# Scales of the weights: one small operation a turn, and the values' maxima two steps sooner

## The chip, the cores and the metric

The kernel runs on one core of a Trainium2 chip. The metric is the device time of one execution in microseconds; the figure before is the median of three runs. Everything else is read from one profiled execution, whose own time stands in the table below. Engine names are those of the profile: PE multiplies matrices, DVE reduces and transposes, ACT exponentiates, POOL does element-wise work, SP issues most DMAs.

## The reference

Two attention blocks A and B over the same input, mixed row by row by a gate (S = 2048 rows, D = 640, 32 heads of 20):

```python
def block(x, wqkv, wo):
    q, k, v = split_heads(x @ wqkv)          # 32 heads of 20
    p = softmax(q @ k.T * 20 ** -0.5)
    return (p @ v).reshape(B, S, D) @ wo

g = sigmoid((x * gate_w).sum(-1, keepdims=True))
out = g * block(x, A_wqkv, A_wo) + (1 - g) * block(x, B_wqkv, B_wo)
```

## The kernel before

The 64 heads of both blocks are worked in 16 groups of four (g = 0 to 15). A group has four blocks of 512 queries, and each of these eight steps over the keys, so the main loop has 512 steps (G), some 5.2 us each; step G belongs to group G // 32. In a step PE makes eight score products (L672), which ACT exponentiates (L675), and two sets of eight value products into the one accumulator bank `acc` (L690), which DVE empties with a transpose `ot` (L777) every eighth step. Some 15 steps ahead of the scores PE makes the same products the other way round (L614), and DVE takes each row's maximum from them: six plain reductions a step (L625) and one fused operation (L622, two records), whose other half ACT has rectified first (L618). Products and their readers share seven PSUM banks. Beside this, the projections of later groups (L407) fill one or two slots a step.

Each weight block is split in two f16 halves after division by a power of two near its largest magnitude, so that maximum has to be known first. The chain that finds it runs three times for queries and keys (`scales_qk`), seven times for values (`scales_v`, one for each group pair gg = 1 to 7) and twice for the output weights (`scales_o`): twelve times in the main loop. It goes so:

- the weights are loaded into `wstage` (one of two buffers) and DVE takes each partition's maximum. For values this is one reduction of 128x800, `m` (L258); for the others it is pieces, `wmax`.
- `scales_by_dram` (L201 on): SP writes the 128 maxima to DRAM (L208), reads them back to every partition as `srows` (L212), and DVE reduces them to `es` (L216).
- `powers` (L165 on): four operations on `es` (L168 to L171) make the power of two and its inverse. The second and third each read what the one before wrote; the fourth reads the second's result.
- `then`: copies and products for the kind of chain. For values `r_v` (L233) and two or three pieces of `wrow` (L239); for queries and keys `r_qk` (L226) and three operations on `esc` (L228 to L230); for output weights `r_o` and two operations on `f_o` (L251 to L253).

The order of instructions on each engine is the order in which the Python code emits them. A chain is a generator on a list `side`; `advance()` moves every generator of it by one `yield`, and it is called eight times a step, after each score product. What stands between two yields is emitted as one piece. The table of future work is filled by `at(G, task)`; its tasks run in the middle of step G, after the fourth score product and ahead of the second set of value products. For values and group g = 2gg - 2, which begins at step b = 32g, the load is put at b - 9, the maximum at b - 6 and the split of the weights at b - 1. For gg = 1, whose b is 0, these are steps 0, 3 and 8, and for gg = 7 load and maximum come by a rule of their own, at 338 and 341. `take_acc`, which issues `ot`, runs right after the second set of value products of every step that 8 divides.

The banks are chosen by `take()`, which picks the bank that a running tally of engine times (`spend`, `tick_block`) holds to be free first. The tally counts 0.5 us for a maximum of weights and 0.35n + 0.5 us for a whole chain's tail, at the place of its `es` reduction.

Of the kernel before, what the change touches and what calls it, by code (L numbers as in the profile page):

```python
# [12 lines left out]
I32 = mybir.dt.int32  # L13
# [11 lines left out]
NT = S // P  # L25
# [46 lines left out]
def kernel(  # L72
# [73 lines left out]
    def give(i, t):  # L146
        free_at[i] = t
        held.discard(i)
# [7 lines left out]
    def tick_block(cost, ready=0.0):  # L156

        begin = block_end[0] if now[0] < 0 and block_end[1] == rows_free else max(rows_free) + T_MODE
        clock["pe"] = max(begin, ready)
        rows_free[:] = [clock["pe"] + cost + T_MODE] * 2  # L160
        block_end[:] = [clock["pe"] + cost, list(rows_free)]
        clock["done"] = clock["pe"] + cost + T_READY - T_MODE


    def powers(ei, n):  # L165

        c = [slice(k * n, (k + 1) * n) for k in range(5)]
        nc.vector.tensor_scalar(ei[:, c[1]], ei[:, c[0]], 0x7F800000, None, op0=OP.bitwise_and)  # L168
        nc.vector.tensor_scalar(ei[:, c[2]], ei[:, c[1]], float(20 << 23), None, op0=OP.max)
        nc.vector.tensor_scalar(ei[:, c[3]], ei[:, c[2]], -1.0, float((254 + XE) << 23), op0=OP.mult, op1=OP.add)  # L170
        nc.vector.tensor_scalar(ei[:, c[4]], ei[:, c[2]], float(XE << 23), None, op0=OP.subtract)  # L171

    def scales(maxima, n, then):

        for _ in range(REST):
            yield
        yield PRODUCT
        i, pt = take()
        nc.tensor.transpose(pt[:n, :P], maxima[:, :n], ident)
        tick_block(0.1, free_at[i])  # L180
        yield
        e = wts.tile([5, 8], F32, name="e", tag="scl", bufs=2)
        nc.vector.tensor_reduce(e[:n, 0:1], pt[:n, :P], axis=AX.X, op=OP.max)
        give(i, spend("dve", 0.3, clock["done"]))
        spend("dve", 1.0)
        powers(e.bitcast(I32)[:n, :], 1)
        dg = wts.tile([5, 10], F32, name="dg", tag="scd", bufs=2)[:n, :2 * n]
        nc.vector.tensor_tensor(dg.rearrange("p (k n) -> p k n", k=2), ident[:n, :n].unsqueeze(1).to_broadcast([n, 2, n]),
                                e[:n, 3:5].unsqueeze(2).to_broadcast([n, 2, n]), op=OP.mult)
        for _ in range(REST):  # L190
            yield
        yield PRODUCT
        i, pb = take()
        tick_block(0.1, free_at[i])
        nc.tensor.matmul(pb[:, :2 * n], ones[:n, :], dg, start=True, stop=True)
        yield
        both = wts.tile([P, 10], F32, name="both", tag="scb", bufs=2)
        nc.vector.tensor_copy(both[:, :2 * n], pb[:, :2 * n])
        give(i, spend("dve", 0.2, clock["done"]))
        then(both[:, :n], both[:, n:2 * n])  # L200

    def scales_by_dram(maxima, n, then):

        turn = next(scale_turns)
        flat = s_scr[turn % 3][:n * P]
        yield
        yield
        nc.sync.dma_start(flat.rearrange("(p n) -> p n", n=n), maxima[:, :n])  # L208
        for _ in range(STORED):
            yield  # L210
        rows = wts.tile([P, 2 * P], F32, name="srows", tag="srows", bufs=2)[:, :n * P]
        nc.sync.dma_start(rows, flat.unsqueeze(0).to_broadcast([P, n * P]))  # L212
        for _ in range(LOADED):
            yield
        e = wts.tile([P, 10], F32, name="es", tag="ses", bufs=2)
        nc.vector.tensor_reduce(e[:, :n], rows.rearrange("p (q n) -> p n q", n=n), axis=AX.X, op=OP.max)  # L216
        spend("dve", 0.35 * n + 0.5)
        powers(e.bitcast(I32), n)
        then(e[:, 3 * n:4 * n], e[:, 4 * n:5 * n])

    def set_x(r_x, r, inv):
        nc.vector.tensor_copy(r_x, r)
# [1 line left out]

    def set_qk(i, r, inv):
        nc.vector.tensor_copy(r_qk[i], r)  # L226
        e = esc[i]
        nc.vector.tensor_tensor(e, inv[:, 0:1], inv_x, op=OP.mult)  # L228
        nc.vector.tensor_scalar(e, e, inv[:, 1:2], float(DH ** -0.5 / QKS ** 2), op0=OP.mult, op1=OP.mult)
        nc.vector.tensor_tensor(e, e, inv_x, op=OP.mult)  # L230

    def set_v(gg, r, inv):
        nc.vector.tensor_copy(r_v[gg], r)  # L233

        f = gg % (NG // 2) * 160
        while f < (gg % (NG // 2) + 1) * 160:
            p0 = f % P
            n = min(P - p0, (gg % (NG // 2) + 1) * 160 - f, (P, 32, 64, 32)[p0 // 32])
            nc.vector.tensor_copy(wrow[gg // (NG // 2)][p0:p0 + n, f // P:f // P + 1], inv[p0:p0 + n])  # L239
            f += n  # L240

    def scales_qk(i, maxima):
# [6 lines left out]
    def scales_o(z, maxima):  # L249
        def then(r, inv):  # L250
            nc.vector.tensor_copy(r_o[z], r)  # L251
            nc.vector.tensor_scalar(f_o[z], gates[:, z, :], inv, inv_x, op0=OP.mult, op1=OP.mult)
            nc.vector.tensor_scalar(f_o[z], f_o[z], 1.0 / QKS, None, op0=OP.mult)  # L253

        return scales_by_dram(maxima, 1, then)
# [49 lines left out]
    side = []  # L305
# [139 lines left out]
    def run(gen):  # L445
        for _ in gen:
            pass
# [468 lines left out]
    load, split_next = weights_a(1)  # L916
# [4 lines left out]
    r, inv = found  # L921
# [72 lines left out]
    rv, invv = of_v  # L994
# [5 lines left out]
    run(r_chunk(1, (0, 1)))  # L1000

    def next_group():
        set_qk(0, r[:, 0:2], inv[:, 0:2])
        set_v(0, rv[:, 0:1], invv[:, 0:1])
        split_next()
        yield True

# [30 lines left out]
    todo, fill, current = {}, [], []  # L1038

    def at(G, f):  # L1040
        todo.setdefault(G, []).append(f)
# [5 lines left out]
    def tasks(G, gap, fs):  # L1047
        for k, f in enumerate(fs):
            at(G + k * gap, f)

    at(4, sigmoids)
    step = NQ * NS
    for g in range(2 * NG):
        b = g * step
        n = g + 1
        if n < 2 * NG:
            parts = APARTS.get(n, 3)
            fill += [((-8, 15)[g] if g < 2 else b + AFROM, b + ADUE + ADUES * ch if g else 4 + 3 * ch, parts, project_a(n, ch))
                     for ch in range(4)]
            if n + 1 < 2 * NG:  # L1060
                tasks(b + 2 if g else 9, 3, weights_a(n + 1))
            i = g // 4 + 1
            if i < 4:
                if g % 4 == 0:
                    z, c0 = i // 2, 320 * (i % 2)
                    srcs = max_tasks([[(wqkv[z], part * D + c0 + 160 * k) for k in range(2)] for part in range(2)],
                                     lambda m, i=i: scales_qk(i, m))
                    tasks(b + QKMAX[i], 2, srcs)
                if g % 4 == 2:
                    tasks(b + 6, 3, weights_r(i))  # L1070
                    parts = RPARTS.get(i, 3)
                    fill += [(b + 12, b + 26 + 6 * ch if i == 1 else b + 22 + 4 * ch, parts, project_r(i, ch)) for ch in range(4)]
            gg = g // 2 + 1
            if gg < NG and g % 2 == 0:
                load, scale, split = weights_v(gg)
                at(max(b - 9, 0), load)
                if gg < NG - 1:
                    at(max(b - 6, 3), lambda scale=scale: side.append(scale()))
                at(max(b - 1, 8), split)
                fill += [(max(b + 2, 10), b + 2 * step - 4 + j // 2, 2, project_v(gg, j)) for j in range(0, NT, 2)]  # L1080
    early = weights_v(NG - 1)
    at(VEARLY, early[0])
    at(VEARLY + 3, lambda: side.append(early[1]()))
# [89 lines left out]
    for G in range(STEPS + 1):  # L1173
# [13 lines left out]
        for what in (STEP[blocks] if maxima or some else LATE + " X" * (blocks == 2)).split():  # L1187
            k = count[what] = count.get(what, 0) + 1
            if what[0] == "e":
                q = sum(count.get(f"e{j}", 0) for j in range(2)) - 1  # L1190
                j = int(what[1])
# [55 lines left out]
```

## Time and profile before

| | |
|---|---|
| median of three runs | 2762.35 us (2762.08 to 2764.07) |
| the profiled execution | 2762.97 us |
| its span | 2761.2 us |
| PE, busy share of the span | 99% |
| ACT | 92% |
| DVE | 89% |
| POOL | 24% |

The profiled execution lies 0.62 us above the median and within the three runs. Its span is 1.8 us shorter than its time; nothing of that lies in the main loop. A start of a row is counted from the span's start. Two DVE operations may overlap by some hundredths in their records, since an operation's record goes on after the next one has begun; the distance of two starts is what one costs the engine. PE's records overlap likewise, so that PE counts as busy in places where it advances slowly; how far it advances is read from the starts of its rows. A set of value products is eight rows of L690, merged to one with x8.

### The profile page before, as it was taken

What the parts mean: (1) busy time and instruction counts of PE and PEld (TensorE: products, weight loads), DVE (VectorE), ACT (ScalarE), POOL (GpSimd) and SP (SyncE); (2) the same over time, 40 slices, a digit from 0 to 9 for tenths busy, and PEclk for the clock granted to TensorE, in tenths of its full rate; (3) what the DMA queues carried; (4) which work ended last, traced back from release to release, by engine and by line L of the source; (5) the groups of instructions that cost most, each with busy time, mean ns of one, the idle gap of its engine ahead of it and who ended that gap; (6) DMA issues with size and microseconds to landing.
All of it is one profiled execution on the core that took longest, in us unless ns stands there. A gap on an engine that the chain in (4) does not pass through costs nothing.

```text
span 2761.2 us, 62247 instructions
## 1 busy us (share of the span) xinstructions
PE 2722.8 (99%) x23273; PEld 935.9 (34%) x23273; DVE 2444.3 (89%) x4785; ACT 2528.5 (92%) x5128; POOL 667.0 (24%) x909
## 2 busy tenths in 40 slices
PE   7999999999999999999999999999999999999998
PEld 3433333333333332333333333333333333333222
DVE  7789899999999989888888998989988898999982
ACT  4999999999999999999999999999999999999987
POOL 6232222222123421311221111222342202100111
PEclk8999999999999999999999999999999999999999
DMA  4021102010120211102012230221201112132112
GB/s 143 16 57 26 31 11 47 7 31 16 25 55 20 60 42 49 43 9 61 20 45 62 60 85 25 60 56 48 65 17 42 30 50 63 32 78 63 47 48 76
DMA packets 176432, 125.58 MB, mean 45 GB/s; under 512 B 105216, under 2 KB 145976, under 8 KB 176128
## 3 DMA queue, kind: packets, MB, share of 16 engines
q1 hardware_dynamic: 173584, 119.99, 17.1%
q8 instruction: 182, 2.98, 0.5%
q0 software_dynamic: 1600, 0.96, 0.2%
q14 instruction: 122, 1.00, 0.1%
q10 hardware_dynamic: 944, 0.66, 0.1%
HBM read 55.53 MB, written 31.86 MB: 32 GB/s over the span
## 4 chain that ended last, share of the span: by engine, by line
PE 94%; DVE 4%; ACT 1%; DMA 1%; issue 0%; POOL 0%; POOLq 0%; SPq 0%; ACTq 0%; DVEq 0%
PE acc L690 35%; PE bank L407 20%; PE bank L614 20%; PE bank L672 18%; DVE mpart L625 2%; ACT pt L675 1%; DMA ws<-in_A_wqkv_dram 0%; PE bank L854 0%; DVE rl L622 0%; PE bank L900 0%; DVE ot L777 0%; DMA xs<-in_A_x_dram 0%; POOL wstage L336 0%; ACT rl L618 0%; DVE es L216 0%
## 5 line engine op out<-in xcount | busy, mean ns | idle before, releaser
L675 ACT ACTIVATE pt<-bank 128x512 f32<-128x512 f32 x4096 | 2168.5, 613 | 146.0 <-PE bank L672 98.0
L625 DVE TENSOR_REDUCE mpart<-bank 128x1 f32<-128x512 f32 x2944 | 1843.7, 682 | 220.4 <-PE bank L614 118.8
L690 PE MATMUL acc<-pt,v 128*21 128x512 f32 x8192 | 1081.7, 600 | 1.4 <-DVE ot L777 1.2
L672 PE MATMUL bank<-qt,kt 64*128 64x512 f16 x4096 | 1041.7, 380 | 4.6 <-DVE mpart L625 2.9
L614 PE MATMUL bank<-kt,qt 60*128 60x512 f16 x3520 | 1011.6, 380 | 4.2 <-ACT pt L675 1.3
L614 PEld LDWEIGHTS <-qt 60*128 60x128 f16 x4096 | 238.4, 94 | 883.4 <-issue 821.9
L622 DVE CUSTOM_DVE_ANT_0 rl<-bank,rl 128x512 f32<-128x512 f32 x576 | 388.1, 680 | 7.0 <-ACT rl L618 2.2
L618 ACT ACTIVATE rl<-bank 128x512 f32<-128x512 f32 x576 | 336.9, 594 | 7.1 <-PE bank L614 6.7
L672 PEld LDWEIGHTS <-kt 64*128 64x128 f16 x4096 | 230.2, 94 | 199.4 <-issue 88.5
L690 PEld LDWEIGHTS acc<-pt,v 128*21 128x21 f32 x8192 | 143.0, 99 | 431.9 <-issue 426.4
L407 PE MATMUL bank<-xx,wbh 128*128 128x168 f16 (+3 forms) x2480 | 287.7, 236 | 1.4 <-DVE wbh L926 1.0
L407 PE MATMUL bank<-xx,wbl 128*128 128x168 f16 (+3 forms) x1240 | 257.5, 235 | 0.0
L785 POOL TENSOR_TENSOR ot<-ot,sq 128x512 f32<-128x512 f32 x63 | 66.0, 1048 | 755.3 <-DVE sq L782 755.3
L407 PEld LDWEIGHTS <-wbh 128*128 128x128 f16 x2480 | 192.8, 98 | 110.8 <-issue 104.5
L614 PE MATMUL bank<-kd,qt 60*128 60x512 f16 x576 | 203.7, 379 | 0.1
L407 PE MATMUL bank<-woh,o_in 128*128 128x320 f16 (+3 forms) x700 | 157.7, 290 | 0.0
L407 PE MATMUL bank<-wvh,xx 128*128 128x160 f16 (+1 forms) x1280 | 156.7, 234 | 0.6 <-DVE mpart L622 0.6
L436 POOL CAST cq<-fs 128x512 f16<-128x512 f32 x60 | 36.6, 610 | 477.3 <-ACT fs L434 473.6
L407 PEld LDWEIGHTS <-xx 128*128 128x128 f16 x1920 | 131.1, 97 | 59.1 <-issue 56.3
L407 PE MATMUL bank<-wvl,xx 128*128 128x160 f16 (+1 forms) x640 | 137.7, 232 | 0.0
L407 PEld LDWEIGHTS <-wbl 128*128 128x128 f16 x1240 | 121.1, 98 | 4.7 <-issue 1.3
L407 PEld LDWEIGHTS <-o_in 128*128 128x128 f16 (+1 forms) x1050 | 87.3, 97 | 90.7 <-issue 68.8
(145 smaller groups left out, 1247.4 us busy)
## 6 DMA issues: line engine op xcount, KB each, us to landing
y_scr<-y_out SPq DMA_DIRECT2D x48, 320.0 KB
y_out<-y_scr SPq DMA_DIRECT2D x32, 320.0 KB
kt<-cq SPq DMA_DIRECT2D x120, 80.0 KB
o_scr<-on SPq DMA_DIRECT2D x240, 40.0 KB
o_in<-o_scr SPq DMA_DIRECT2D x64, 96.0 KB
kt<-cq SPq DMA_DIRECT2D x136, 40.0 KB
wstage<-in_B_wqkv_dram SPq DMA_DIRECT2D x13, 400.0 KB
xs<-in_A_x_dram SPq DMA_DIRECT2D x8, 640.0 KB
```

Source lines behind the costliest of these rows:

```text
L407: nc.tensor.matmul(out_ap, a, b, start=(k == 0), stop=(k == len(pairs) - 1))
L436: nc.gpsimd.tensor_copy(hi, f)
L614: nc.tensor.matmul(pt, QT[g % 2][r, pair, q0:q0 + P], k, start=True, stop=True)
L618: nc.scalar.activation(relus[u, j], pt, AF.Relu)
L622: nc.vector.tensor_tensor_reduce(rl, pt, rl, 1.0, LOW, OP.add, OP.max, m)
L625: nc.vector.tensor_reduce(m, pt, axis=AX.X, op=OP.max)
L672: nc.tensor.matmul(et, KT[g % 2][r, pair, kt * P:(kt + 1) * P], QT[g % 2][r, pair, qb * QB:(qb + 1) * QB], start=True, stop=True)
L675: nc.scalar.activation(pt, et, AF.Exp, scale=factor(g // 4))
L690: nc.tensor.matmul(acc[32 * h:32 * h + VW, :], V[(g // 2) % 2][:, kt, (g % 2) * GH + h, :], ptiles.pop((G, kk, h)), start=(kt == 0), stop= ...
L785: nc.gpsimd.tensor_tensor(t3, t3, sq.unsqueeze(2).to_broadcast([P, 16, 32]), op=OP.mult)
```

## The change

`powers` and each `then` yield after nearly every operation, so that a chain's tail of eight or nine operations is emitted over several turns of `advance()`, with other work between them. Calls at the start, outside the main loop, are run through at once as before. The values' load and maximum are put two steps sooner, and for gg = 1 the split and the projection it feeds are allowed two steps later.

```diff
         nc.vector.tensor_scalar(ei[:, c[1]], ei[:, c[0]], 0x7F800000, None, op0=OP.bitwise_and)
+        yield
         nc.vector.tensor_scalar(ei[:, c[2]], ei[:, c[1]], float(20 << 23), None, op0=OP.max)
+        yield
         nc.vector.tensor_scalar(ei[:, c[3]], ei[:, c[2]], -1.0, float((254 + XE) << 23), op0=OP.mult, op1=OP.add)
+        yield
         nc.vector.tensor_scalar(ei[:, c[4]], ei[:, c[2]], float(XE << 23), None, op0=OP.subtract)
+        yield
...
         spend("dve", 0.35 * n + 0.5)
-        powers(e.bitcast(I32), n)
-        then(e[:, 3 * n:4 * n], e[:, 4 * n:5 * n])
+        yield
+        yield from powers(e.bitcast(I32), n)
+        yield from then(e[:, 3 * n:4 * n], e[:, 4 * n:5 * n])
...
     def set_v(gg, r, inv):
         nc.vector.tensor_copy(r_v[gg], r)
+        yield
...
             nc.vector.tensor_copy(wrow[gg // (NG // 2)][p0:p0 + n, f // P:f // P + 1], inv[p0:p0 + n])
+            yield
...
-                at(max(b - 9, 0), load)
+                at(max(b - 11, 0), load)
                 if gg < NG - 1:
-                    at(max(b - 6, 3), lambda scale=scale: side.append(scale()))
-                at(max(b - 1, 8), split)
-                fill += [(max(b + 2, 10), b + 2 * step - 4 + j // 2, 2, project_v(gg, j)) for j in range(0, NT, 2)]
+                    at(max(b - 8, 3), lambda scale=scale: side.append(scale()))
+                at(max(b - 1, 10), split)
+                fill += [(max(b + 2, 12), b + 2 * step - 4 + j // 2, 2, project_v(gg, j)) for j in range(0, NT, 2)]
```

`set_qk` and `then` of `scales_o` have yields in the same manner.

What this does to the order of the engines, at three places. A row has the line, the operation and the tiles; lines of the change count from the changed file, so L216 there is L220, L258 is L270, L625 is L637, L622 is L634 and L777 is L789. `ISA` is the fused operation and the read of its result.

DVE, the tail of the chain of gg = 3, before (some 125 steps in):

```order
L625 TENSOR_REDUCE mpart<-bank_93 128x1
L216 TENSOR_REDUCE es<-srows 128x1
L168 TENSOR_SCALAR es<-es 128x1
L169 TENSOR_SCALAR es<-es 128x1
L170 TENSOR_SCALAR es<-es 128x1
L171 TENSOR_SCALAR es<-es 128x1
L233 COPY r_v_110<-es 128x1
L239 COPY wrow_115<-es 32x1
L239 COPY wrow_115<-es 128x1
L622 ISA rl,mpart<-bank_92,rl 128x512
```

DVE, the same tail in the change, from its third operation on (the reduction and three maxima stand ahead of it):

```order
L168 TENSOR_SCALAR es<-es 128x1
L170 TENSOR_SCALAR es<-es 128x1
L634 ISA rl,mpart<-bank_91,rl 128x512
L634 ISA mpart 128x1
L172 TENSOR_SCALAR es<-es 128x1
L174 TENSOR_SCALAR es<-es 128x1
L637 TENSOR_REDUCE mpart<-bank_95 128x1
L241 COPY r_v_110<-es 128x1
L248 COPY wrow_115<-es 32x1
L637 TENSOR_REDUCE mpart<-bank_89 128x1
L248 COPY wrow_115<-es 128x1
```

Eight operations in a row have become five groups of one or two, with one to three maxima between them, and the whole stands two steps sooner.

DVE, around the transpose of the accumulator eight steps ahead of gg = 3's group (step 120), in the change:

```order
L637 TENSOR_REDUCE mpart<-bank_93 128x1
L270 TENSOR_REDUCE m_9810<-wstage 128x1
L634 ISA rl,mpart<-bank_94,rl 128x512
L634 ISA mpart 128x1
L789 STREAM_TRANSPOSE ot<-acc 128x512
L794 RECIPROCAL sq<-ot 128x16
L637 TENSOR_REDUCE mpart<-bank_89 128x1
```

Before, `m` stood two steps later, and these rows stood here without it. Since b - 8 is divisible by eight, `m` now comes in the step of `ot`, directly ahead of it, for gg = 2, 3, 4, 5 and 6.

DVE, the same place for gg = 4 (step 184), in the change:

```order
L270 TENSOR_REDUCE wmax<-wstage 128x1
L270 TENSOR_REDUCE m_14336<-wstage 128x1
L637 TENSOR_REDUCE mpart<-bank_92 128x1
L637 TENSOR_REDUCE mpart<-bank_95 128x1
L634 ISA rl,mpart<-bank_91,rl 128x512
L634 ISA mpart 128x1
L270 TENSOR_REDUCE wmax<-wstage 128x1
L789 STREAM_TRANSPOSE ot<-acc 128x512
L794 RECIPROCAL sq<-ot 128x16
```

Here `m` joins the last two pieces of the queries' and keys' maxima; they stood here before, `m` did not. Further on, the chain of gg = 4 and that of queries and keys i = 2, which followed each other without a row between them, are a step and a half apart.

On PE and ACT the order of instructions is the same in both kernels; only which bank a product takes differs, and whose product had that bank before differs in five short stretches, where `m` has moved. On POOL the split of gg = 1 comes five rows later. On SP the load of `wstage` comes one to three rows sooner in two places, and the read of `srows` directly behind the write of the maxima, ahead of the DMAs of the row maxima (L646, L650), in four.

More of the change, by code (lines that the diff above doesn't have):

```diff
@@ L185, in scales @@
         spend("dve", 1.0)
-        powers(e.bitcast(I32)[:n, :], 1)
+        run(powers(e.bitcast(I32)[:n, :], 1))
         dg = wts.tile([5, 10], F32, name="dg", tag="scd", bufs=2)[:n, :2 * n]
@@ L226, in set_qk @@
         nc.vector.tensor_copy(r_qk[i], r)
+        yield
         e = esc[i]
         nc.vector.tensor_tensor(e, inv[:, 0:1], inv_x, op=OP.mult)
+        yield
         nc.vector.tensor_scalar(e, e, inv[:, 1:2], float(DH ** -0.5 / QKS ** 2), op0=OP.mult, op1=OP.mult)
+        yield
         nc.vector.tensor_tensor(e, e, inv_x, op=OP.mult)
@@ L233, in set_v @@
         nc.vector.tensor_copy(r_v[gg], r)
+        yield
         f = gg % (NG // 2) * 160
@@ L239, in set_v @@
             nc.vector.tensor_copy(wrow[gg // (NG // 2)][p0:p0 + n, f // P:f // P + 1], inv[p0:p0 + n])
+            yield
             f += n
@@ L251, in then @@
             nc.vector.tensor_copy(r_o[z], r)
+            yield
             nc.vector.tensor_scalar(f_o[z], gates[:, z, :], inv, inv_x, op0=OP.mult, op1=OP.mult)
+            yield
             nc.vector.tensor_scalar(f_o[z], f_o[z], 1.0 / QKS, None, op0=OP.mult)
@@ L1002, in next_group @@
     def next_group():
-        set_qk(0, r[:, 0:2], inv[:, 0:2])
-        set_v(0, rv[:, 0:1], invv[:, 0:1])
+        run(set_qk(0, r[:, 0:2], inv[:, 0:2]))
+        run(set_v(0, rv[:, 0:1], invv[:, 0:1]))
         split_next()
```

## The prediction

> **What bounds the kernel now.** I read the page first, down to its chain that ended last, then the timelines of PE and DVE around single chains.
>
> ```profile
> PE 94%; DVE 4%; ACT 1%; DMA 1%; issue 0%; POOL 0%; POOLq 0%; SPq 0%; ACTq 0%; DVEq 0%
> ```
>
> PE sets the end: 94% of the chain of waits is its own work, and the change leaves that work and its order alone. Only what PE loses by waiting can be won or added, and of that what DVE causes. To see such a loss I compare the distance between the starts of two sets of value products with the same stretch of work elsewhere. PE's timeline (start, length, engine, line, operation, tiles, count), first pair, then the stretch of the first chain (gg = 1), then the last chain's:
>
> ```profile
> 135.00 1.06 PE L690 MATMUL acc<-pt,v 128*21 128x512 f32 x8
> 138.48 1.06 PE L690 MATMUL acc<-pt,v 128*21 128x512 f32 x8
> 140.23 1.05 PE L690 MATMUL acc<-pt,v 128*21 128x512 f32 x8
> 144.32 1.06 PE L690 MATMUL acc<-pt,v 128*21 128x512 f32 x8
> ...
> 1979.36 1.06 PE L690 MATMUL acc<-pt,v 128*21 128x512 f32 x8
> 1982.17 1.06 PE L690 MATMUL acc<-pt,v 128*21 128x512 f32 x8
> ```
>
> A long stretch (ten score products and a projection of 168 columns) takes 3.48 us undisturbed, a short one (six score products, no projection) 138.48 to 140.23, 1.75 us. Where the first chain's tail runs, the long one takes 4.09: PE loses 0.61. Where the last runs, the short one takes 2.81: 1.06 lost. The twelve chains lie at eleven places (two follow each other at 1072); read in the same way, each against a stretch with the same products, they lose 0.61, 0.45, 0.49, 0.29, 0.35, 1.97 (the pair, over three stretches), 0.51, 0.62, 0.69, 0.78 and 1.06: **7.8 us** in all. That is the most the first half of the change can win.
>
> How a tail costs PE its time is seen at gg = 3, on DVE and on PE:
>
> ```profile
> 738.43 0.68 DVE L622 CUSTOM_DVE_ANT_0 rl<-bank,rl 128x512 f32<-128x512 f32 x1
> ...
> 739.49 1.29 DVE L625 TENSOR_REDUCE mpart<-bank 128x1 f32<-128x512 f32 x2 [0.36 <-PE bank L672]
> ...
> 743.41 0.28 DVE L216 TENSOR_REDUCE es<-srows 128x1 f32<-128x128 f32 x1
> 743.72 0.15 DVE L168 TENSOR_SCALAR es<-es 128x1 int32<-128x1 int32 x1
> ...
> 744.09 0.15 DVE L170 TENSOR_SCALAR es<-es 128x1 int32<-128x1 int32 x1
> 744.16 0.14 DVE L171 TENSOR_SCALAR es<-es 128x1 int32<-128x1 int32 x1
> ...
> 744.70 0.68 DVE L622 CUSTOM_DVE_ANT_0 rl<-bank,rl 128x512 f32<-128x512 f32 x1
> ...
> 745.31 3.68 DVE L625 TENSOR_REDUCE mpart<-bank 128x1 f32<-128x512 f32 x6
> ```
>
> ```profile
> 396.43 1.06 PE L690 MATMUL acc<-pt,v 128*21 128x512 f32 x8
> 399.66 1.06 PE L690 MATMUL acc<-pt,v 128*21 128x512 f32 x8
> ...
> 743.05 1.06 PE L690 MATMUL acc<-pt,v 128*21 128x512 f32 x8
> 746.05 0.37 PE L672 MATMUL bank<-qt,kt 64*128 64x512 f16 x1
> 746.57 0.63 PE L690 MATMUL acc<-pt,v 128*21 128x512 f32 x4
> ```
>
> The tail holds DVE from 743.41 to 744.70, 1.29 us. In the rhythm without it the first maximum behind a fused operation starts 1.06 after that operation (738.43 to 739.49), of which 0.36 is waiting for PE; it would start at 743.41 + 1.06 = 744.47 and starts at 745.31, 0.84 late. It ends at 745.99, and PE's product at 746.05 takes the bank then. PE loses 3.52 - 3.23 = 0.29. So **some 0.55 us of lateness are forgiven** by the seven banks with this projection of 128 columns; what lies above goes into PE's time one to one.
>
> **The change part by part.**
>
> *The tails, spread.* An operation that reads its predecessor's result starts 0.18 to 0.19 after it (743.72 to 744.09 for two of them); the fourth (744.16), which doesn't need the third, 0.07 after it. The same price is paid by a small operation between strangers:
>
> ```profile
> 1053.03 0.15 DVE L300 TENSOR_REDUCE m<-wmax 128x2 f32<-128x8 f32 x1
> 1053.10 0.98 DVE L258 TENSOR_REDUCE m<-wstage 128x1 f32<-128x800 f32 x1
> 1053.99 0.68 DVE L622 CUSTOM_DVE_ANT_0 rl<-bank,rl 128x512 f32<-128x512 f32 x1
> ```
>
> 0.07 for the small one, 0.89 for `m`. In the new order of gg = 3: reduction 0.28 - 0.07 = 0.21, the pair L168/L170 0.19 + 0.07, L172/L174 0.14, `r_v` and the first `wrow` 0.14, the last `wrow` 0.07: 0.82 in place of 1.29. And it comes in portions: the fused operation is 0.47 late, the next maximum 0.61 less the 0.36 of waiting, 0.25, the one behind it 0.39, then 0.46 less the next wait. All below 0.55, so PE should lose nothing. Queries' and keys' tails have a reduction twice as wide and one operation more, and their first two operations adjoin; by the same prices they reach some 0.6. The two chains from 1890 on start in steps with `ot` or with the row maxima's finish, where DVE is late already. For these five I keep 0.2 each, 1.0 in all: **6.8 us won**. Bounds: 7.8 if nothing is left; 4.2 if the operations keep the price of a dependent pair (a rival, below).
>
> [...]
>
> *`m`, two steps sooner.* This is where the change pays. In the step of `ot` before, gg = 3 again:
>
> ```profile
> 712.26 0.68 DVE L622 CUSTOM_DVE_ANT_0 rl<-bank,rl 128x512 f32<-128x512 f32 x1
> ...
> 713.02 0.72 DVE L777 STREAM_TRANSPOSE ot<-acc 128x512 f32<-128x512 f32 x1
> ...
> 713.95 3.68 DVE L625 TENSOR_REDUCE mpart<-bank 128x1 f32<-128x512 f32 x6
> ```
>
> The first maximum would start at 712.26 + 1.06 = 713.32 and starts 0.63 late, just about forgiven. With `m` ahead of the fused operation all comes 0.89 later, less the 0.07 that `ot` waits for PE now: 1.45 late. The projection there has 160 columns. From 128 to 168 columns a stretch grows by 3.48 - 3.23 = 0.25, to 160 by 0.20; that much longer the banks have, so 0.75 is forgiven and 0.70 lost. I take this for gg = 3, 5 and 6; for gg = 2, with 128 columns, 1.45 - 0.55 = 0.90. At gg = 4 PE waits for `ot` itself already:
>
> ```profile
> 1040.43 0.64 DVE L258 TENSOR_REDUCE wmax<-wstage 128x1 f32<-128x480 f32 x1
> ...
> 1043.19 0.71 DVE L777 STREAM_TRANSPOSE ot<-acc 128x512 f32<-128x512 f32 x1
> ```
>
> ```profile
> 1043.95 1.06 PE L690 MATMUL acc<-pt,v 128*21 128x512 f32 x8 [0.87 <-DVE ot L777]
> ```
>
> There `m` goes in behind the row at 1040.43 and its 0.89 fall to PE whole. Sum: 3 x 0.70 + 0.90 + 0.89 = 3.9. At their old places these five cost little: at gg = 2
>
> ```profile
> 401.41 1.06 PE L690 MATMUL acc<-pt,v 128*21 128x512 f32 x8
> 405.13 1.06 PE L690 MATMUL acc<-pt,v 128*21 128x512 f32 x8
> ```
>
> 3.72 - 3.23 = 0.49, at the others under 0.1. Net **3.4 us given back**. Bounds: -0.5 (the banks are chosen anew around `m`, and the tally knows 0.5 of its 0.89), and 8.6 (the slower rival).
>
> *Queues.* The loads issue two steps sooner into a buffer whose reader is done by then, since the next `wstage` is wanted before and after in the same turn of two. `srows` now stands ahead of the row maxima's DMAs on SP:
>
> ```profile
> 723.83 0.35 SPq L208 DMA_DIRECT2D s_scr<-m  x1
> 724.27 1.78 SPq L646 DMA_DIRECT2D m_scr<-m4r  x4
> ```
>
> ```profile
> SPq L212 <- DMA s_scr<-m: 17.9, 3, 8.3
> ```
>
> The maxima will be written some 10 us sooner, near 713.9; even the longest wait for their landing, 8.3, ends by 722.3, before the issue at 724.27 is due. Cost nothing; were that cover gone, L650 would come later by the rest, against scores that by the code's lead are some seven steps off.
>
> *The split of gg = 1.* POOL makes `wvl` five rows later:
>
> ```profile
> 145.26 2.29 POOL L336 TENSOR_SCALAR wstage<-wstage,r_v 128x800 f32<-128x800 f32 x1
> ...
> 148.55 1.67 POOL L339 TENSOR_TENSOR wvl<-wstage,wvh 128x800 f16<-128x800 f32 x1
> ...
> 155.47 0.30 POOL L642 TENSOR_TENSOR m4r<-mt,m4r 128x64 f16<-128x64 f32 x1
> ```
>
> ```profile
> 163.49 0.23 PE L407 MATMUL bank<-wvl,xx 128*128 128x160 f16 x1
> ```
>
> The three operations took 145.26 to 150.22, 5.0; starting behind 155.8 they end near 160.8, 2.7 ahead of PE's first use. Nothing.
>
> **The sum**: -6.8 + 3.4 = -3.4. Against the profiled execution's 2762.97 that is 2759.6; the median of the runs lies 0.62 lower, so I forecast **2758.9**.
>
> **The rivals.**
>
> *The moved maxima cost nothing.* The new choice of banks steers PE past the late ones, or more is forgiven than I read from one stretch. For it: 0.63 late cost nothing in any step of `ot`. Against: gg = 4 waits for the accumulator, not for a bank. -6.8 - 0.5 = -7.3: 2755.1.
>
> *Spread, but not cheaper.* Each small operation keeps some 0.19. Then the maximum behind the fused operation is about 0.6 late and the next about 1.0, up to 0.45 above what is forgiven; with some 0.3 left in each of twelve chains, 3.6, the change wins 4.2 and gives back 3.4, -0.8 in all: 2761.5. Against it: 1053.03 to 1053.10. [...]
>
> *Slower: the lateness of `m` is paid again.* Behind `ot` come, in the next steps, the finish of the row maxima and the transpose back:
>
> ```profile
> L788 DVE STREAM_TRANSPOSE ob<-ot 128x512 f32<-128x512 f32 x63 | 44.2, 702 | 0.0
> L632 DVE TENSOR_REDUCE mneg<-mpart 128x16 f32<-128x64 f32 x64 | 14.0, 219 | 5.8 <-POOL mpart L596 0.5
> ```
>
> If DVE hasn't caught up by then, PE pays for each of them too: 0.9 + 0.22 + 0.70, about 1.8 at each of the five places, 9.1 in all. Less 0.49 at the old ones that is 8.6 against 6.8 won, +1.8: 2764.2. It decides where the waits of DVE for PE (0.36 at 739.49) are gone for two steps in a row. Against: PE's own halt gives DVE that time.
>
> *Nothing happens*: 2762.4; only if DVE's lateness weren't what PE waited for, and 746.05 says it is.
>
> **How the numbers follow.** Forecast 0.55, maxima free 0.22, not cheaper 0.13, slower 0.08, nothing 0.02. The range goes from the free maxima to just past the median before: 2755.0 to 2762.8. What a measurement of this kernel can tell from no change is about 0.2%, 5.5 us: below 2756.8 lie the free maxima and the forecast's low tail, 0.30; above 2767.9 only the far end of the slower case, 0.05; the rest, 0.65, is within.
>
> **What would show it.** In the profile after: small DVE operations at 0.07 from the next start; no stretch over its plain length at the tails; at the five places of `m` ahead of `ot` a stretch longer by 0.7 to 0.9, and at gg = 4 a wait for `ot` of about 1.75 in place of 0.87. It is wrong if the tails still cost PE 0.3 each, if the five stretches are plain, or if PE loses time in the two steps behind them.

## The result, and the profile after

| | before | change |
|---|---|---|
| median of 22 runs each | 2762.86 us (2762.07 to 2764.49) | 2759.54 us (2759.02 to 2761.23) |
| the profiled execution | 2762.97 us | 2759.30 us |
| its span | 2761.2 us | 2757.5 us |
| first set of value products in the main loop starts at | 105.78 | 105.17 |
| from there to the last set but two | 2634.86 | 2631.70 |

The ratio is 0.9988 [0.9982, 0.9993]: the change is 3.3 us faster, less than the 0.2% that a measurement of this kernel was taken to tell from no change, though with 22 runs the interval does not contain 1. The forecast was 2758.9. The last row is the sum of 1,021 distances, each from the start of one set of eight value products (L690, in the change L702) to the start of the next; the two distances behind them, 0.87 and 2.00, are alike in all runs and left out. Since PE's order is the same in both kernels, each distance of the one has its partner in the other, and their difference says where the time went. The loop itself is **3.16 us shorter**; ahead of it the change's execution is another 0.61 shorter (105.78 to 105.17), of which 0.1 is lost again behind the loop.

The page after, its chain of waits:

```profile
PE 94%; DVE 3%; ACT 1%; DMA 1%; issue 0%; POOL 0%; POOLq 0%; SPq 0%; DVEq 0%; ACTq 0%
```

DVE's share of the chain has gone from 4% to 3%. What PE waited for is told more finely by the view of waits. Before (engine, line, releaser: us in total, times, longest):

```profile
PE bank L672 <- DVE mpart L625: 2.9, 9, 0.7
...
PE acc L690 <- DVE ot L777: 1.2, 3, 0.9
...
PE bank L672 <- ACT pt L675: 0.8, 3, 0.4
```

and the same view after:

```profile
PE bank L684 <- DVE mpart L637: 2.0, 7, 0.6
PE acc L702 <- DVE ot L789: 1.6, 3, 1.3
PE bank L684 <- ACT pt L687: 1.6, 5, 0.5
```

The scores' recorded waits for DVE's maxima fell from 2.9 to 2.0 us, those of the value products for `ot` rose by 0.4, and the scores' waits for ACT doubled, from 0.8 to 1.6. The records show only a part of what PE loses, because its rows overlap; the sums by starts are larger, but have the same shape.

**The tails.** PE's timeline after, at the first chain's place and at gg = 3's old one:

```profile
139.62 1.06 PE L702 MATMUL acc<-pt,v 128*21 128x512 f32 x8
143.09 1.06 PE L702 MATMUL acc<-pt,v 128*21 128x512 f32 x8
...
742.25 1.06 PE L702 MATMUL acc<-pt,v 128*21 128x512 f32 x8
745.48 1.06 PE L702 MATMUL acc<-pt,v 128*21 128x512 f32 x8
```

The long stretch takes 3.47 where it took 4.09, the other 3.23 where it took 3.52: both are at their plain lengths. The tail of gg = 3 now begins at 730.55. DVE's timeline there:

```profile
730.55 0.28 DVE L220 TENSOR_REDUCE es<-srows 128x1 f32<-128x128 f32 x1
730.75 1.88 DVE L637 TENSOR_REDUCE mpart<-bank 128x1 f32<-128x512 f32 x3
732.54 0.14 DVE L168 TENSOR_SCALAR es<-es 128x1 int32<-128x1 int32 x1
732.72 0.15 DVE L170 TENSOR_SCALAR es<-es 128x1 int32<-128x1 int32 x1
732.79 0.68 DVE L634 CUSTOM_DVE_ANT_0 rl<-bank,rl 128x512 f32<-128x512 f32 x1
...
733.39 0.15 DVE L172 TENSOR_SCALAR es<-es 128x1 int32<-128x1 int32 x1
733.46 0.14 DVE L174 TENSOR_SCALAR es<-es 128x1 int32<-128x1 int32 x1
733.52 0.68 DVE L637 TENSOR_REDUCE mpart<-bank 128x1 f32<-128x512 f32 x1
```

L168 and L170, of which one reads the other's result, are 0.18 apart; L170, L172 and L174 cost 0.06 or 0.07 from start to start. The first five operations take 0.20 + 0.25 + 0.13 = 0.58 of DVE in three portions.

**The moved maxima.** DVE and then PE at gg = 3's step of `ot`:

```profile
711.25 0.97 DVE L270 TENSOR_REDUCE m<-wstage 128x1 f32<-128x800 f32 x1
712.14 0.68 DVE L634 CUSTOM_DVE_ANT_0 rl<-bank,rl 128x512 f32<-128x512 f32 x1
...
712.75 0.71 DVE L789 STREAM_TRANSPOSE ot<-acc 128x512 f32<-128x512 f32 x1
...
713.67 1.82 DVE L637 TENSOR_REDUCE mpart<-bank 128x1 f32<-128x512 f32 x3
```

```profile
710.89 1.06 PE L702 MATMUL acc<-pt,v 128*21 128x512 f32 x8
714.35 0.39 PE L626 MATMUL bank<-kt,qt 60*128 60x512 f16 x2 [0.16 <-DVE mpart L637]
714.67 0.63 PE L702 MATMUL acc<-pt,v 128*21 128x512 f32 x4
```

`m` costs DVE its 0.89 (711.25 to 712.14), and the first maximum behind `ot` would start at 711.25 + 1.06 = 712.31 but starts 1.36 late. Yet the stretch takes 3.78 against 3.62 before: PE loses 0.16, not 0.70. At gg = 4 PE waits for the accumulator:

```profile
1040.11 1.06 PE L702 MATMUL acc<-pt,v 128*21 128x512 f32 x8
...
1043.90 1.06 PE L702 MATMUL acc<-pt,v 128*21 128x512 f32 x8 [1.26 <-DVE ot L789]
...
1045.97 0.37 PE L684 MATMUL bank<-qt,kt 64*128 64x512 f16 x1 [0.47 <-ACT pt L687]
```

From 2.90 before to 3.79, 0.89 more, `m` whole; of it 0.39 show as a longer wait (1.26 for 0.87) and the rest as slower progress ahead of it. The next stretch is 0.47 longer too, behind ACT.

All differences above 0.06, put together by what lies there (us, change less before):

| what | places (start in the run before) | sum |
|---|---|---|
| tails gone from their old places | 140 -0.61, 259 -0.36, 418 -0.49, 743 -0.29, 865 -0.31, pair at 1072 -1.29, 1412 -0.52, 1749 -0.69, 1890 -0.78, 1979 -1.06 | -6.40 |
| more won beside them | 1586 -0.34, 1739 -0.21, 423 -0.11, 722 -0.07, 1728 -0.08 | -0.81 |
| new at and behind the tails | 869 +0.81; gg = 2's tail at 407 to 413 +0.77; 262 +0.19; 733, 1063, 1401, 1892, 1982 +0.64 together | +2.41 |
| `m` | 391 +0.49, 401 -0.49; 712, 1380, 1718 +0.16 each; 1041 +0.90 and the next +0.47 | +1.85 |
| neither | 520 +0.19, 925 -0.35, 2211 -0.11 | -0.27 |

With the differences too small to list (+0.06) that is -3.16. One place of the eleven is missing from the first row: at 1582 the stretch takes 3.82 in both kernels, 0.62 over its plain length. And of gg = 2's 0.49 at 418 nothing is won in the end, since as much is lost at the tail's new place.

### The profile page after: what moved, and what is told of

The parts are those of the page before. It is cut to its first block, busy times and chain, and to the rows that moved or that the text cites. A ratio compares the mean times of both kernels' runs of the same rounds, so it can differ in the third digit from the quotient of the medians.

```text
span 2757.5 us, 62235 instructions
## 1 busy us (share of the span) xinstructions
PE 2720.0 (99%) x23273; PEld 937.6 (34%) x23273; DVE 2441.9 (89%) x4785; ACT 2528.3 (92%) x5128; POOL 666.6 (24%) x909
## 3 DMA queue, kind: packets, MB, share of 16 engines
q14 instruction: 123, 1.01, 0.1%
## 4 chain that ended last, share of the span: by engine, by line
PE 94%; DVE 3%; ACT 1%; DMA 1%; issue 0%; POOL 0%; POOLq 0%; SPq 0%; DVEq 0%; ACTq 0%
PE acc L702 35%; PE bank L419 20%; PE bank L626 20%; PE bank L684 18%; DVE mpart L637 2%; ACT pt L687 1%; DMA ws<-in_A_wqkv_dram 0%; PE bank L866 0%; DVE rl L634 0%; DVE ot L789 0%; PE bank L912 0%; DMA xs<-in_A_x_dram 0%; DVE m L270 0%; ACT rl L630 0%; DVE wmax L270 0%
## 5 line engine op out<-in xcount | busy, mean ns | idle before, releaser
L637 DVE TENSOR_REDUCE mpart<-bank 128x1 f32<-128x512 f32 x2944 | 1845.7, 682 | 221.3 <-PE bank L626 120.3
L702 PE MATMUL acc<-pt,v 128*21 128x512 f32 x8192 | 1081.7, 600 | 1.7 <-DVE ot L789 1.6
L634 DVE CUSTOM_DVE_ANT_0 rl<-bank,rl 128x512 f32<-128x512 f32 x576 | 387.8, 679 | 6.8 <-ACT rl L630 2.4
L702 PEld LDWEIGHTS acc<-pt,v 128*21 128x21 f32 x8192 | 143.0, 99 | 427.6 <-issue 421.6
```

The costliest lines, as they stand in the source:

```text
L634: nc.vector.tensor_tensor_reduce(rl, pt, rl, 1.0, LOW, OP.add, OP.max, m)
L637: nc.vector.tensor_reduce(m, pt, axis=AX.X, op=OP.max)
L702: nc.tensor.matmul(acc[32 * h:32 * h + VW, :], V[(g // 2) % 2][:, kt, (g % 2) * GH + h, :], ptiles.pop((G, kk, h)), start=(kt == 0), stop= ...
```

## The experiments

Each was timed against the kernel before on the same chip, except two with a single run. For each its length of the loop, from the first set of value products on, is given as in the table above (before 2634.86, change 2631.70); it leaves out the start, which differs from execution to execution.

**The spread tails alone**, with the values' load and maximum at their old steps:

```diff
-                at(max(b - 11, 0), load)
+                at(max(b - 9, 0), load)
-                    at(max(b - 8, 3), lambda scale=scale: side.append(scale()))
+                    at(max(b - 6, 3), lambda scale=scale: side.append(scale()))
```

> The small operations spread as in the change, the values' loads and maxima at their old steps (b - 9, b - 6). Two separate terms (my theory): the tails alone win what the trace of the change shows at their places, 4.6 us of PE time, and nothing is given back at the steps of ot: 4 to 5.5 us below the kernel before, about 2758, and 1 to 2 us below the change. Rival, the gain comes from the tails' new places: less than 2 us below before. At gg = 4 the two tails fall together again; if each portion is small enough PE still loses under 0.5 there (1.97 before).

Measured 2759.5 against 2762.55, ratio 0.9987 [0.9978, 0.9996]; the loop is 2631.26, 3.60 shorter than before and only 0.44 shorter than the change. That is less than was expected of it. The pair of tails at 1072 still costs 1.25 where under 0.5 was expected, and two stretches near gg = 6's place grew (+0.52 at 1737 and +0.39 at 1751 of its execution). At gg = 2's old place nothing is won: the stretch that took 3.34 with the tail in one piece takes 3.34 with the tail spread (417.45 to 420.79; plain is 2.85).

**The moved maxima alone**: the kernel before with the change's loads, maxima and split, and the tails in one piece.

> The values' loads and maxima two steps sooner, the tails in one piece as before. My theory: PE loses 0.9 more at gg = 4's accumulator, 0.49 more at gg = 2, 0.16 more at gg = 3, 5 and 6, and wins 0.49 at gg = 2's old place: 1.2 to 2 us slower than before where the tails cost at the new places what they cost at the old ones. The pair of tails at 1072 is parted here too: up to 1 us may come back by that. In all 0 to +2 us. Rival, the moved maxima are free or win: -1 or below.

Measured 2766.12 against 2762.55, ratio 1.0011 [1.0002, 1.0020]; the loop is 2638.83, 3.97 longer, more than the 0 to 2 that were expected. The stretches of `ot` cost what they do in the change (+0.49 at gg = 2, +0.16 at gg = 3, 5 and 6, +0.89 at gg = 4). But the one-piece tails cost more at the new places than they did at the old ones: 0.89, 0.66, 1.05 and 0.89 for gg = 3 to 6, where the old places gave back 0.29 to 0.69. PE at gg = 3:

```profile
730.49 1.05 PE L690 MATMUL acc<-pt,v 128*21 128x512 f32 x8
732.83 0.37 PE L672 MATMUL bank<-qt,kt 64*128 64x512 f16 x1 [0.53 <-DVE mpart L625]
733.13 1.06 PE L690 MATMUL acc<-pt,v 128*21 128x512 f32 x8
```

2.64 in place of the plain 1.74; in the change the same stretch, with the spread tail in it, takes 1.74 (730.25 to 731.99).

Not all of the 3.97 is waiting, though. The two stretches behind gg = 4's took 4.35 and 5.13, where the change has 3.83 and 3.61: 2.04 more, with no wait for DVE to go with it. Eight value products took 1.91 there (at 1048.78) in place of 1.06, and the view of windows shows a lower clock; the last three numbers of a row are the granted clock of PE, the DMA share and GB/s. In this execution:

```profile
1044.00:1052.00 8.00, 7.31 (x32) 1.36 (x33) 5.74 (x12) 3.71 (x8) 1.10 (x2) 0.58 0.01 4
```

The granted clock was 0.58 in these 8 us, right behind PE's wait of 1.26 for `ot`; in the change's execution it was 1.00. Without these 2.0 the moved maxima cost some 1.9. So the halves still don't add, but by less than the lengths say: -3.60 and +1.9 make -1.7, and together they are -3.16. On the kernel before the move costs some 1.9 us; on one with spread tails, 0.4 (2631.70 against 2631.26).

**Four more operations in each tail, in a row**, on the kernel before. Each reads and writes the same element, so that the result stays.

```diff
         nc.vector.tensor_scalar(ei[:, c[1]], ei[:, c[0]], 0x7F800000, None, op0=OP.bitwise_and)
+        for _ in range(4):
+            nc.vector.tensor_scalar(ei[:, c[1]], ei[:, c[1]], 0x7F800000, None, op0=OP.bitwise_and)
```

> The kernel before with four further small operations in each powers, each reading the result of the one ahead. By the price of a dependent pair (0.19 from start to start) each tail is 0.75 longer. My theory, lateness beyond what is forgiven goes to PE one to one: 0.75 at each of eleven to twelve places, 8 to 9 us, and about 1.3 us at the start where two chains run with PE waiting: 9 to 11 us slower than before. Rival, there is slack that the tails haven't used up: under 5 us slower.

**The same four in the change, each in a turn of its own** (the loop has a `yield` ahead of each).

> The change with the same four further operations, each a turn of its own. My theory, a small operation between others costs 0.07 to 0.19 and is forgiven in its rhythm: 0 to 2 us more than the change in the loop, plus about 1.3 us at the start. Rival, each operation keeps its price and delays PE wherever it stands: 8 us or more above the change.

Measured 2773.18 and 2763.2 against 2762.55, ratios 1.0037 [1.0023, 1.0050] and 1.0001 [0.9991, 1.0010]. In a row the four make the loop 8.8 us longer than before, 0.71 to 0.81 at nearly every place; spread, 2.1 longer than the change, in which 0.81 are a gain at 867 (there two other operations come free of POOL, see below), so that the four themselves cost 2.9. PE at gg = 3's place, in a row and then spread:

```profile
746.40 1.06 PE L692 MATMUL acc<-pt,v 128*21 128x512 f32 x8
...
750.66 1.06 PE L692 MATMUL acc<-pt,v 128*21 128x512 f32 x8
```

```profile
744.18 1.06 PE L705 MATMUL acc<-pt,v 128*21 128x512 f32 x8
747.41 1.06 PE L705 MATMUL acc<-pt,v 128*21 128x512 f32 x8
```

4.26 where the kernel before had 3.52: 0.74 for four operations at 0.19, so all of the added lateness goes into PE's time once the banks' slack is used. Spread, 3.23: nothing. This is the clearest proof of the prediction's first mechanism. It isn't free everywhere: at 146, 262 and 416 the spread four cost 0.4 to 0.5, and at 1074 0.8. At 262 and 1074 single small operations of the tail took up to 0.72 and 1.50 us and ended 0.02 and 0.03 behind an operation of POOL.

**The maxima unknown to the tally of engine times**, in the change. The table of banks is made with 0 for `m` instead of 0.5:

```diff
-    def largest(dst, src):
+    def largest(dst, src, cost=0.5):
-        spend("dve", 0.5)
+        spend("dve", cost)
-            largest(m, st["t"])
+            largest(m, st["t"], 0.0)
```

> The change with the values' maximum counted at 0 in the tally of engine times that chooses the banks (0.5 in the change). My theory, the forgiven lateness at the steps of ot is larger than I read (1.2 in place of 0.75) because the tally steers PE off the banks that come late: without it PE loses 0.5 to 0.7 at gg = 3, 5 and 6 (0.16 in the change). Rival, the banks' choice doesn't matter there: 0.16 as in the change.

**The same with 1.0** for `m`, nearly its true 0.89:

> The change with the values' maximum counted at 1.0 us, near the 0.89 it takes. My theory: PE loses no more than 0.16 at gg = 3, 5 and 6, and perhaps nothing; gg = 4, where PE waits for the accumulator and not for a bank, keeps its 0.9. Rival: no difference to the change.

One run each: 2762.37 and 2759.66. With 0 the loop is 2634.91, 3.2 longer than the change, and PE at gg = 3 shows why:

```profile
711.42 1.06 PE L702 MATMUL acc<-pt,v 128*21 128x512 f32 x8
713.42 0.23 PE L419 MATMUL bank<-wvh,xx 128*128 128x160 f16 x1 [0.40 <-DVE mpart L634]
715.77 1.06 PE L702 MATMUL acc<-pt,v 128*21 128x512 f32 x8
```

The stretch takes 4.35, which is 0.73 over the 3.62 of the kernel before; the same at gg = 5 and 6. The engines do the same work in the same order, only the banks differ, and the lost time comes near the 0.70 that the prediction gave this place. With 1.0 the loop is 2631.57, and 0.14 are lost there in place of the change's 0.16: counting 0.5 does as well as counting 1.0. (0.26 of the blind kernel's 3.2 lie at 1045, where the granted clock fell to 0.50 again.)

**The last operations of the output weights' tail, seven turns after the copy** instead of one. In the change the stretch after 867.79 grew by 0.81. DVE and POOL there:

```profile
867.43 0.70 DVE L263 TENSOR_SCALAR f_o<-gates,es,inv_x 128x16 f32<-128x16 f32 x1
...
868.65 0.72 DVE L265 TENSOR_SCALAR f_o<-f_o 128x16 f32<-128x16 f32 x1
```

```profile
867.50 0.61 POOL L448 CAST cq<-fs 128x512 f16<-128x512 f32 x1 [14.93 <-ACT fs L446]
868.19 1.16 POOL L449 TENSOR_TENSOR cq<-fs,cq 128x512 f16<-128x512 f32 x1
```

In the kernel before the same two took

```profile
866.91 0.28 DVE L252 TENSOR_SCALAR f_o<-gates,es,inv_x 128x16 f32<-128x16 f32 x1
867.23 0.17 DVE L253 TENSOR_SCALAR f_o<-f_o 128x16 f32<-128x16 f32 x1
```

and POOL's cast came behind them, at 868.59. Now the first ends at 868.13, 0.02 behind the cast (868.11), and the second at 869.37, 0.02 behind POOL's next operation (869.35). The theory was that DVE stands behind POOL here; the edit moves the two away from it:

```diff
             nc.vector.tensor_copy(r_o[z], r)
-            yield
+            for _ in range(7):
+                yield
             nc.vector.tensor_scalar(f_o[z], gates[:, z, :], inv, inv_x, op0=OP.mult, op1=OP.mult)
```

> The change with seven turns in place of one between r_o and the first operation on f_o, so that on the chain at 865 both operations on f_o come behind POOL's two operations (867.50 to 869.35 in the trace of the change). My theory, DVE stands still on these two operations (0.70 and 0.72 us recorded, 0.28 and 0.17 in the kernel before) because POOL works on SBUF at the same time: the two are back at 0.3 and 0.2 and PE's 0.81 at that place are gone, so 0.8 us below the change. Rival, it is their place between maxima: they stay long, and PE still loses there.

Measured 2759.52 against 2762.32, ratio 0.9990 [0.9981, 0.9999]; the loop is 2631.66, as the change's. The place itself did what was expected: the two operations take 0.28 and 0.17 and the stretch 1.75, so the 0.81 are gone. But the second chain of output weights now meets POOL in its turn: its operation L266 at 1984.93 takes 0.64 and ends at 1985.57, and POOL's L805, from 1984.38 on, ends at 1985.53. The stretch there is 0.51 longer. The collision moved, and with it most of the loss.

**Other steps for the chains**, to get the maxima out of the step of `ot`. First the spread tails with the old steps of the values, and the other chains a step later:

```diff
-QKMAX = (0, 10, 42, 10)
+QKMAX = (0, 11, 43, 11)
-OMAX, OSPLIT = (134, 346), (151, 362)
+OMAX, OSPLIT = (135, 346), (152, 362)
```

> The tails spread, the values' maxima at their old steps, and the maxima of queries, keys and the first output weights one step later, so that none of them falls into a step of ot. In the kernel before PE loses 0.63, 0.69, 0.68, 0.29, 1.16 + 0.51 and 0.34 at the six steps where they do, 4.3 in all. My theory, that loss is ot behind a maximum, and goes: 3 to 4.3 us below the run with the spread tails alone, about 2756. Rival, the maxima cost the same in any step: no difference to that run.

Measured 2758.02 against 2762.32, ratio 0.9984 [0.9975, 0.9993], loop 2629.60. That is 1.7 below the loop of the tails alone, where 3 to 4.3 were expected. Some losses only moved (+0.88 at 1075, +0.62 at 1551).

Then the change with the values' load and maximum one step later, at b - 10 and b - 7, with `QKMAX` (0, 11, 42, 10) and the output weights as above:

> The change with the values' maxima at b - 7, one step later than in the change and out of the step of ot, and the maxima of keys i = 1 and of the first output weights one step later as well; i = 2 and 3 as before. My theory, place by place from the runs so far: the maxima at the steps of ot no longer cost 0.49, 0.16 x 3 and 0.9 + 0.47 (2.3), the shifted ones win another 0.6 and 0.6, and the chain at 865 misses POOL (0.8): some 4 us below the change, 2755 to 2756. Rival, each shift only moves the loss to another step, as it partly did in the run with all maxima on odd steps: 2757.5 or above.

Measured 2758.86 against 2762.28, ratio 0.9986 [0.9977, 0.9995], loop 2630.32; that is the rival's case, 2757.5 or above. +1.09 at 1075 ate much of what `m` gave back, and DVE and POOL show what it is:

```profile
1073.57 1.24 DVE L172 TENSOR_SCALAR es<-es 128x2 int32<-128x2 int32 x1
```

```profile
1073.12 1.67 POOL L351 TENSOR_TENSOR wvl<-wstage,wvh 128x800 f16<-128x800 f32 x1
```

A small operation of the tail, 0.17 us long elsewhere, lasts until 1074.81, 0.02 after POOL's end (1074.79), and the chain of waits there goes through it. The +0.88 at 1075 in the run before this one has the same cause (1.24 for the same operation). So it is not the old loss in a new step: POOL's work on gg = 4's weights, which waits for the shifted tail's `r_v`, now runs into the tail of i = 2. And the same with 43 in place of 42:

> The same with the maxima of i = 2 one step later too, so that gg = 4's step of ot has no maximum of weights at all. My theory: PE's 1.16 + 0.51 there (trace before) go in part, 0.5 to 1 us below the run with i = 2 at its place. Rival, the pieces in the steps behind cost as much: no difference.

Measured **2756.86** against 2762.28 (11 runs, 2755.75 to 2758.66), ratio 0.9978 [0.9969, 0.9987], loop 2628.83: 2.9 shorter than the change and 6.0 shorter than before, the best of all. In gg = 4's step of `ot`, in which neither `m` nor a piece of the queries' and keys' maxima stands any more, PE's stretch (1039.92 to 1041.87) takes 1.95 in place of 3.79, and the next is 0.91 shorter; 1.24 of these 2.75 come back in the two stretches behind.

## Why the prediction was right, point by point

- **The sum was right, -3.4 against -3.3, and no rival's case came.** 0.5 us of what separates 2758.9 from 2759.54 is the first median, of three runs; over 22 it stands at 2762.86, and the profiled execution is not 0.6 but 0.1 above it. Both terms, however, were too large, by 2.0 and 1.6, and that their errors cancelled is luck.
- **Tails, 6.8 predicted, 4.8 won** (the rows on the tails above: -6.40, -0.81 and +2.41). Reading the losses as lateness of DVE above what the banks forgive held for most of them: the four operations added in a row went into PE's time one to one, and at ten of the eleven old places the loss went down, at gg = 2 only to come back at the new one. The step that failed is "PE should lose nothing": it asked only whether DVE comes too late. At 1582 the same 3.82 remain. ACT and PE there, before and then in the change:

```profile
1581.76 3.77 ACT L675 ACTIVATE pt<-bank 128x512 f32<-128x512 f32 x7 [0.21 <-PE bank L672]
```

```profile
1585.42 0.54 PE L614 MATMUL bank<-kt,qt 60*128 60x512 f16 x2 [0.19 <-DVE mpart L625]
```

```profile
1580.90 3.77 ACT L687 ACTIVATE pt<-bank 128x512 f32<-128x512 f32 x7 [0.20 <-PE bank L684]
```

```profile
1584.72 0.37 PE L626 MATMUL bank<-kt,qt 60*128 60x512 f16 x1 [0.25 <-ACT pt L687]
```

  In the change PE's last product starts 0.05 after ACT's seventh operation ends (1584.67). In the kernel before ACT ends just as late in the stretch, at 1585.53, and PE's second product of the row, 0.37 long, starts at 1585.59, 0.06 after it. The tail's lateness let go of PE at the same time (1585.42 for the first product), so two waits of one length stood there, and taking away DVE's left ACT's. At gg = 2 it was ACT alone already: in the kernel before ACT's operations end at 420.00 and 420.49,

```profile
419.90 0.59 ACT L618 ACTIVATE rl<-bank 128x512 f32<-128x512 f32 x1
```

```profile
420.54 0.37 PE L672 MATMUL bank<-qt,kt 64*128 64x512 f16 x1
```

  and PE's products start 0.05 after each, at 420.05 and 420.54. With the tail spread at the same place the products start as far apart and the stretch takes the same 3.34. So 1.1 of the 7.8 could not be won by a faster DVE, and a look at ACT in the trace before would have shown it. A third part, 0.81, is DVE standing behind POOL, which no part of the prediction weighed.
- **The price of a small operation** was right for those on `es`: 0.06 to 0.07 between strangers, 0.18 for a pair that depends on each other (733.39 to 733.52, and 732.54 to 732.72). The rival "spread, but not cheaper" is out: four more operations cost 8.8 us in a row and 2.9 spread. At gg = 3 `r_v` and the first piece of `wrow`, on 32 partitions, were dearer: 0.17 and 0.19 from start to start (734.12, 734.29 and 734.48) where the prediction took 0.14 for the two.
- **`m`, 3.4 predicted net, 1.85 paid.** At gg = 4 the 0.89 was right to 0.01. At gg = 3, 5 and 6 the term was 0.70 and 0.16 was paid, at gg = 2 0.90 and 0.49. The step that failed is the slack of 0.75, and it failed twice. The prediction took the 0.63 of lateness in the step of `ot` as just forgiven and added 0.20 for the wider projection. PE before shows the stretch of `ot` at gg = 3 and, a step later, one with the same products:

```profile
711.90 1.06 PE L690 MATMUL acc<-pt,v 128*21 128x512 f32 x8
...
715.52 1.06 PE L690 MATMUL acc<-pt,v 128*21 128x512 f32 x8
717.27 1.06 PE L690 MATMUL acc<-pt,v 128*21 128x512 f32 x8
720.70 1.06 PE L690 MATMUL acc<-pt,v 128*21 128x512 f32 x8
```

  3.62 against 3.43: 0.19 of the 0.63 were lost already, and only 0.44 were forgiven. The run with the blind tally agrees: there the first maximum comes 1.36 late, as in the change (at 714.20, where 711.78 + 1.06 is the rhythm), and 4.35 - 3.43 = 0.92 are lost, 0.44 forgiven. What `m` adds is then 1.36 - 0.63 = 0.73, and that the prediction's 0.70 comes near it, from 1.45 - 0.75, is luck. With `m` in the tally 3.78 - 3.43 = 0.35 are lost and 1.01 forgiven. The prediction had named this as a bound ("the banks are chosen anew around `m`") and not taken it. What it left out on the other side are the 0.47 behind ACT in the stretch after gg = 4's.
- **The signs of "what would show it"** came out mixed. Operations at 0.07: yes, but for `r_v` and some pieces of `wrow`. No stretch over its plain length at the tails: at most places. Stretches longer by 0.7 to 0.9 at the places of `m`: only at gg = 4. The wait for `ot` of about 1.75: no, 1.26, since PE had come up to it more slowly.
- **The two halves were summed as if each stood alone.** On the kernel before, the move costs some 1.9, on the spread tails 0.4, since a one-piece tail costs more at the new places. The prediction had looked at what `m` does at its new place and not at what the tail, which moves with it, does there.
- **Queues and the split of gg = 1 at nothing**: no stretch at 145 to 165 differs by more than 0.06, and none shows a wait for the row maxima's DMAs.
- The slower rival, lateness of `m` paid again in the next steps, could be seen only at gg = 4 (+0.47), and there PE waits for ACT and not for the operations that the rival named.

What stays open is why PE waits for a bank of ACT's just there. The wait goes where the tail goes: in the first run with other steps, which has the maxima of i = 3 a step later, the stretch at 1578.25 is plain (3.21) and the one a step behind it takes 3.82 with ACT last, and gg = 2's 3.34 stand at 417.45, 412.63 or 407.53 in the runs with its maximum at b - 6, b - 7 and b - 8. The tally counts a whole tail at its `es` in the change too; whether that entry leads PE to banks that ACT empties late was not run.

## What to carry to other kernels

Small dependent operations on DVE, busy for 89% of the span, cost 0.06 or 0.07 us each where other work stood between them and 0.18 behind one another, as long as POOL didn't hold them up: where it did, two operations on `f_o` took 0.70 and 0.72 in place of 0.28 and 0.17. In one piece the tail cost PE 0.3 or 0.9 us depending on the stretch it fell into. Before summing a gain over places, ask at each of them which engine comes last when this one is on time, and whether the operations meet a neighbour that holds up their engine. Where a planner picks buffers from a tally of costs, ask what a new operation costs once it is entered there: here it was 0.16 instead of 0.73.

## What the runs showed of the hardware

Some DVE operations ended just behind one of POOL's and took longer. In the change L263 and L265, 128x16 f32, took 0.70 and 0.72 us while a POOL operation was running, and each ended 0.02 after POOL's did; in the kernel before, with none beside them, the same two took 0.28 and 0.17 (at 866.91 and 867.23). A third case, the 0.64 of the run with `f_o` later, ended 0.04 after. The run with four spread operations and the first two with other steps have nine more such cases among the operations on `es` with two elements a partition, of 0.25 to 1.50 us in place of 0.17. Not every operation was held up: in the run with `f_o` later L264, 128x16 too, began at 1984.13 in the midst of POOL's cast (1983.69 to 1984.30) and took 0.29. Operations on `es` and copies with one element a partition were not held up: in the change twelve that ran beside an operation of POOL took 0.13 to 0.15, one of them `wrow` at 735.20, 0.15 in the midst of POOL's operation from 734.37 to 736.65. The product into `esc` at 260.72, one element a partition as well, took 0.50 in place of 0.15 and ended 0.01 after POOL's cast (261.22 and 261.21). DVE's maxima, which read PSUM, kept their 0.60 from start to start in the midst of the same POOL operations (868.05 to 868.65). What decides which operation is held up was not shown.

The start differs from one execution to another by as much as a term of this sum, and the granted clock goes with it. With the same instructions ahead of the main loop, its first set of value products started at 104.79 (`f_o` later), 105.17 (the change), 106.03 (tails alone) and 106.36 (the best kernel). The windows from 26 to 30 us of the first and the last:

```profile
26.00:30.00 4.00, 4.00 (x24) 3.01 (x23) 4.00 (x9) 3.45 (x6) 3.92 (x4) 0.76 0.00 0
```

```profile
26.00:30.00 4.00, 4.00 (x16) 2.90 (x15) 4.00 (x8) 2.94 (x5) 3.88 (x4) 0.50 0.02 0
```

The clock rises from 0.50 to 1.00 earlier in the one than in the other; the change (0.66) and the tails alone (0.50) lie between in the same order, the tails alone with 0.94 against the best kernel's 0.86 in the next four us. In the loop the clock fell in three of the profiled executions, each time about a halt of PE (1.26 for `ot` with the maxima alone, 1.24 with the blind tally, 1.71 with four more operations in a row): each has windows of two us at 0.50 behind it, from 1046, 1046 and 1084 on. But the change has the halt of 1.26 with a clock of 1.00, so a halt of that length alone doesn't bring it about; what does was not measured. For small changes this is a reason to compare the lengths of the loop, with the clock beside them, rather than two times.
